# Two heads take turns in the key-value products of a fused attention and MLP kernel, and the second half batch's product moves one step later

## The chip, the cores and the metric

The kernel runs on one core of a Trainium2 chip. The metric is the device time of one execution in microseconds, taken as the median of several runs; lower is better.

## The reference, cut to what matters

Three stages follow one another: a linear attention (softmax over the features of q, softmax over the sequence of k, no product of q with k), a gated MLP with an RMS norm ahead of it, and a second MLP with a rational activation. Shapes: 4 batches, 8 heads, 576 tokens, head size 64; 2304 tokens of width 512; hidden widths 1536 and 2048; all float32.

```python
q_s = softmax(q, axis=-1)                      # over the 64 features of a head
k_s = softmax(k, axis=2)                       # over the 576 tokens
kv  = np.einsum('bhsd,bhse->bhde', k_s, v)     # 64 x 64 for each head: the products of this change
x   = np.einsum('bhsd,bhde->bhse', q_s, kv)    # 2304 x 512 in the end
xn  = x / rms(x) * rms_g
x   = (silu(xn @ w_gate) * (xn @ w_val)) @ w_out
h   = x @ w_in2
out = (P(h) / Q(h)) @ w_out2                   # P, Q: polynomials in h and |h|
```

## The kernel before, in words

The 2304 tokens are cut into six chunks of 384 (numbers c = 0 to 5). The 576 tokens of a batch are laid over 64 partitions times 9 slices, and two heads share the 128 partitions: head h = 0 has partitions 0 to 63, head h = 1 has partitions 64 to 127. A half batch (j = 0 or 1) is four heads: two groups g of two heads h.

**The product.** `kv_pe` makes the four 64x65 results of a half batch (64 columns of v and a column of ones that gives the sum for the softmax). Each is a sum over the 9 slices c, so a product has 2 x 2 x 9 = 36 matmuls of 64 rows, 64 weight columns and 65 moving columns. Both heads write the same PSUM bank, head 0 its partitions 0 to 63, head 1 its partitions 64 to 127. A float32 matmul leaves two records in the trace, so a product shows as x72. `kv_norm` on the VectorE (DVE) then divides by the sums (`rc` is their reciprocal). There are eight products: `akv0`, `akv1` (batch 0) and `bkv0`, `bkv1` (batch 1) in the opening, and two each named `kv_3` and `kv_4` (batches 2 and 3).

**The opening** (about the first 160 us: chunk 0, the loading and splitting of weights, and the attention of chunk 1) runs in the order of a list of names, `ORDER`; each name issues the instructions of one event. The splitting of a weight block into two parts is the work of the lines L169, L174 and L176 (exponents and low words), L183 (`raw`), L190 (`tmp`), L200, L202 and L208 (`w`). The lines `w2` in the list issue two matmuls on an identity (`warm`).

**Chunks 1 to 5** of the first MLP run 12 steps f each: `u_step` issues `g` (12 matmuls), then the events of position 3f, then `vv` (12 matmuls) and the elementwise `product` (u, and its two parts uh by ScalarE and ul by DVE), the events of position 3f + 1, then `y` of the step before (12 matmuls, `emit_y`), then the events of position 3f + 2. While chunk c is worked on, `schedule(c + 1)` puts the attention of the next chunk into these positions; the tuple behind `enumerate` has for each half batch the positions of its maximum, turn, subtraction, exponential and product. Chunk 3 needs batch 2 and chunk 4 needs batch 3, so chunks 2 and 3 have two products each; the other chunks have none there. At position 3 of the tuple, 10, come the exponentials of k and q; at 13 and 15 DVE makes the sums of q (`sumq`) and the normalised q (`qn`); from 18 on q is turned on TensorE (`xq`, which reads `qn`), and from 20 on multiplied with kv (`xx`; the first two use the first half batch's kv, the last two, at 24 and 26, the second's).

All v tiles of the half batches 1 to 3 share one buffer: `load_v(b, 1)` is issued when the first half batch's product has read it. The pool `pw` has four PSUM banks, which g, vv, the products, xq and xx take in turn. Weights for the second MLP are also split in these steps (`stage`, lines L169, L230, L183, L190, L241 and L242).

**After chunk 5** comes the second MLP (`h` and `o` matmuls, 96 steps), bound to TensorE.

Of the kernel before, what the change touches and what calls it, by code (L numbers as in the profile page):

```python
# [47 lines left out]
def kernel(  # L48
# [17 lines left out]
    B, H, S, D = q.shape  # L66
# [5 lines left out]
    SC = S // D  # L72
# [222 lines left out]
    def new_batches(c):  # L295
        return [b for b, off, s, n in runs(c) if s == 0]
# [15 lines left out]
    def load_v(b, j, t=None):  # L312
        t = vt0 if t is None else t
        for g in range(2):
            nc.sync.dma_start(out=t[:, g, :, 0:D], in_=half(v, b, j)[:, g])
        vtl[b, j] = t
# [61 lines left out]
    def kv_pe(b, j, kp):  # L378
        kt, vt = ktl.pop((b, j)), vtl.pop((b, j))
        for g in range(2):  # L380
            for h in range(2):
                r = slice(h * D, (h + 1) * D)
                for c in range(SC):
                    nc.tensor.matmul(
                        kp[r, g * VW:(g + 1) * VW], lhsT=kt[r, g, c], rhs=vt[r, g, c],
                        start=(c == 0), stop=(c == SC - 1),
                    )
# [20 lines left out]
    def q_max(c):  # L408
        mq = at.tile([P, H, TT, 1], F32, tag="mq", name=f"mq_{c}")
        nc.vector.tensor_reduce(out=mq, in_=st["q", c], axis=AX.X, op=ALU.max)  # L410
        st["mq", c] = mq
# [4 lines left out]
    def q_sub(c, eng, i=0, n=1):  # L416
        qt = half_q(st["q", c], i, n)
        eng.tensor_tensor(
            out=qt, in0=qt, in1=half_q(st["mq", c], i, n).to_broadcast(list(qt.shape)), op=ALU.subtract
        )  # L420

    def q_exp(c):
        nc.scalar.activation(st["q", c], st["q", c], AF.Exp)

    def q_sum(c):
        sq = at.tile([P, H, TT, 1], F32, tag="sumq", name=f"sumq_{c}")
        nc.vector.tensor_reduce(out=sq, in_=st["q", c], axis=AX.X, op=ALU.add)
        nc.vector.tensor_scalar_add(sq, sq, 1e-9)
        nc.vector.reciprocal(sq, sq)
        st["sumq", c] = sq  # L430

    def q_norm(c, eng, i=0, n=1):
        if ("qn", c) not in st:
            st["qn", c] = big_tile(F32, xtag[c][0], f"qn_{c}").rearrange(
                "p (t h d) -> p t h d", t=TT, h=H
            )
        qt = half_q(st["q", c], i, n)
        eng.tensor_tensor(
            out=half_q(st["qn", c].rearrange("p t h d -> p h t d"), i, n), in0=qt,
            in1=half_q(st["sumq", c], i, n).to_broadcast(list(qt.shape)), op=ALU.mult,  # L440
        )
# [88 lines left out]
    def rms_wide_pe(c, rp):  # L530
        nc.tensor.matmul(rp[:, :T], lhsT=ones, rhs=st["acc", c], start=True, stop=True)

    def rms_wide(c, rp):
        nv, r, t = (at.tile([P, T], F32, tag=tag, name=f"{tag}w_{c}") for tag in ("sq", "acc", "qT"))
        nc.vector.tensor_scalar(
            out=nv, in0=rp[:, :T], scalar1=-0.5 / DM, scalar2=-0.5e-6, op0=ALU.mult, op1=ALU.add
        )
        nc.vector.tensor_scalar(out=r, in0=nv, scalar1=-2.0, scalar2=None, op0=ALU.mult)
        nc.vector.tensor_scalar(
            out=r.bitcast(I32), in0=r.bitcast(I32), scalar1=-0.5, scalar2=1597463007.0,  # L540
            op0=ALU.mult, op1=ALU.add,
        )
        for _ in range(3):
            nc.vector.tensor_tensor(out=t, in0=r, in1=r, op=ALU.mult)
            nc.vector.tensor_tensor(out=t, in0=t, in1=nv, op=ALU.mult)
            nc.vector.scalar_tensor_tensor(
                out=r, in0=t, scalar=1.5, in1=r, op0=ALU.add, op1=ALU.mult
            )
        st["rms", c] = r
# [26 lines left out]
    def x_norm(c, rp, eng=nc.vector):  # L576
        x_scale(c, 0, rp)
        for p in range(1, KD):
            x_scale(c, p, rp)
            x_rest(c, p - 1, eng)  # L580
        x_rest(c, KD - 1, eng)

    def with_bank(evs, name):

        t = ps(name)
        for pe, _ in evs:
            pe(t)
        for _, rest in evs:
            rest(t)

    def k_events(b, j):
        e = {}
        e["max"] = lambda: k_max(b, j)
        e["turn"] = (lambda t: k_turn_pe(b, j, t), lambda t: k_turn(b, j, t))
        e["sub"] = (lambda t: k_sub_pe(b, j, t), lambda t: k_sub(b, j, t))
        e["exp"] = lambda: k_exp(b, j)
        e["kv"] = (lambda t: kv_pe(b, j, t), lambda t: kv_norm(b, j, t))
        return e

    def x_events(c, p, qT=None):  # L600
        return (
            (lambda t: q_turn_pe(c, p, t), lambda t: q_turn(c, p, t, qT)),
            (lambda t: x_pe(c, p, t), lambda t: x_out(c, p, t)),
        )

    def schedule(c):

        at_pos = [[] for _ in range(NPOS)]

        def put(i, fn):  # L610
            at_pos[i].append(fn)

        def bank(i, ev, name):
            put(i, lambda: with_bank([ev], f"{name}_{c}"))

        eng = nc.gpsimd if c < 2 else nc.vector
        for b in new_batches(c):
            for j, at_ in enumerate(((0, 4, 7, 10, 14), (2, 5, 9, 10, 17))):
                e = k_events(b, j)
                put(at_[0], e["max"])  # L620
                bank(at_[1], e["turn"], f"kt{j}")
                bank(at_[2], e["sub"], f"ks{j}")
                put(at_[3], e["exp"])
                bank(at_[4], e["kv"], f"kv{j}")
                if j == 0:
                    put(at_[4], lambda b=b: load_v(b, 1))
        put(3, lambda: q_max(c))
        put(5, lambda: q_sub(c, eng))
        put(10, lambda: q_exp(c))
        put(13, lambda: q_sum(c))  # L630
        put(15, lambda: q_norm(c, eng))
        turns = []
        for p, (i, n) in enumerate(((18, 20), (20, 22), (22, 24), (24, 26))):
            turn, xev = x_events(c, p)
            bank(n, xev, f"xx{p}")
            turns.append((i, turn, f"xq{p}"))
        for i, turn, name in turns:
            bank(i, turn, name)
        bank(28, (lambda t: rms_wide_pe(c, t), lambda t: rms_wide(c, t)), "rp")
        put(31, lambda: x_norm(c, st["rms", c]))  # L640
        return at_pos
# [181 lines left out]
    with tc.manual_schedule():  # L823
# [73 lines left out]
        for c, pre in enumerate("ab"):  # L897
            for j in range(2):
                put(f"{pre}km{j}", k_max, c, j)
                bank(f"{pre}kt{j}", lambda t, c=c, j=j: k_turn_pe(c, j, t))  # L900
                reader(f"{pre}kx{j}", f"{pre}kt{j}", lambda t, c=c, j=j: k_turn(c, j, t))
                bank(f"{pre}ks{j}", lambda t, c=c, j=j: k_sub_pe(c, j, t))
                reader(f"{pre}kd{j}", f"{pre}ks{j}", lambda t, c=c, j=j: k_sub(c, j, t))
                put(f"{pre}ke{j}", k_exp, c, j)
                put(f"{pre}kz{j}", kv_zero, c, j)
                bank(f"{pre}kv{j}", lambda t, c=c, j=j: kv_pe(c, j, t))
                reader(f"{pre}kn{j}", f"{pre}kv{j}", lambda t, c=c, j=j: kv_norm(c, j, t))
            put(f"{pre}lq", load_q, c)
            put(f"{pre}qm", q_max, c)
            put(f"{pre}qe", q_exp, c)  # L910
            put(f"{pre}qs", q_sum, c)
            for i in range(2):
                for key, fn in (("qd", q_sub), ("qn", q_norm)):
                    name = f"{pre}{key}{i}"
                    put(name, fn, c, engine(name, nc.gpsimd, nc.vector), i, 2)
            for p in range(NP):
                bank(f"{pre}xq{p}", lambda t, c=c, p=p: q_turn_pe(c, p, t))
                bank(f"{pre}xx{p}", lambda t, c=c, p=p: x_pe(c, p, t))
# [145 lines left out]
        for s in range(2, len(steps) + 3):  # L1064
            if s < len(steps):
                c, f = steps[s]
# [44 lines left out]
```

## Time and profile before

| what | value |
|---|---|
| median of 3 runs | 998.48 us (998.29 to 1000.58) |
| profiled execution: its own time | 999.16 us |
| profiled execution: span from first to last instruction | 997.4 us |
| TensorE (PE) busy | 955.3 us, 96% |
| DVE busy | 683.4 us, 69% |
| ScalarE (ACT) busy | 579.5 us, 58% |
| mean granted TensorE clock | 0.985 |

PE is the matmul stream and PEld its weight loads, which lie under it. A share over the whole span hides that the stages differ: the chain of work that ended last goes through DVE in the opening and through PE from about 160 us on.

### The profile page before, as it was taken

How to read it: one execution, taken by the hardware profiler on the slowest of the kernel's cores; microseconds unless marked ns; L12 is line 12 of the kernel's file. 1: busy time of each engine (PE TensorE's matmuls, PEld its weight loads, DVE VectorE, ACT ScalarE, POOL GpSimd, SP SyncE). 2: the span in 40 equal slices, each digit the busy share in tenths (PEclk: the TensorE clock that was granted, in tenths of full speed). 3: DMA queues.
4: the chain of work that ended last, by engine and by line, in shares of the span. 5: the costliest groups of instructions: out<-in, count | busy, mean ns of one | idle time of the engine just before them, and what ended most of it. 6: DMA issues, size and time to landing. Idle time of an engine off the chain costs nothing.

```text
span 997.4 us, 14266 instructions
## 1 busy us (share of the span) xinstructions
PE 955.3 (96%) x5408; PEld 896.3 (90%) x5408; DVE 683.4 (69%) x1160; ACT 579.5 (58%) x1069; POOL 230.8 (23%) x208
## 2 busy tenths in 40 slices
PE   8787879999999999999999999999999999999998
PEld 7676769999989999999999998999999999999997
DVE  5799997577655765666650028877777777777776
ACT  2556554553354235435531238888888788878876
POOL 2475545000000000000001212423323324234222
PEclk9999889999998999999999999999999999999999
DMA  8996001455553645443438731010010010100000
GB/s 209 352 314 221 1 1 53 138 169 179 166 151 104 181 161 147 152 155 127 169 136 307 254 128 64 1 64 1 1 64 1 1 64 1 64 1 1 33 1 32
DMA packets 69588, 108.92 MB, mean 109 GB/s; under 512 B 22672, under 2 KB 49296, under 8 KB 69520
## 3 DMA queue, kind: packets, MB, share of 16 engines
q1 hardware_dynamic: 69520, 108.02, 33.7%
q8 instruction: 42, 0.69, 0.3%
q14 instruction: 26, 0.21, 0.1%
HBM read 79.70 MB, written 28.31 MB: 108 GB/s over the span
## 4 chain that ended last, share of the span: by engine, by line
PE 84%; DVE 12%; issue 2%; DMA 2%; ACT 0%; DVEq 0%
PE h L650 7%; PE o L803 7%; PE h L648 7%; PE o L802 7%; PE h L649 7%; PE o L801 7%; PE g L648 4%; PE g L649 4%; PE g L650 4%; PE vv L648 4%; PE vv L649 4%; PE vv L650 4%; PE y L649 4%; PE y L650 4%; PE y L648 4%; DVE raw L183 3%
## 5 line engine op out<-in xcount | busy, mean ns | idle before, releaser
L789 POOL TENSOR_TENSOR gl<-t,gh 128x384 fp32r<-128x384 f32 x94 | 104.5, 1112 | 253.3 <-ACT gh L787 223.0
L650 PE MATMUL h<-y,wf 128*128 128x384 f32 x384 | 129.5, 337 | 0.0
L648 PE MATMUL h<-y,wf 128*128 128x384 f32 x384 | 129.3, 337 | 0.0
L649 PE MATMUL h<-y,wf 128*128 128x384 f32 x384 | 128.9, 336 | 0.0
L762 DVE SCALAR_TENSOR_TENSOR A<-S,absb,A 128x384 f32<-128x384 f32 x96 | 61.6, 641 | 92.9 <-ACT A L752 92.9
L686 ACT ACTIVATE uh<-u 128x384 fp32r<-128x384 f32 x72 | 37.8, 524 | 133.4 <-DVE u L695 114.3
L803 PE MATMUL o<-wf,gl 128*128 128x512 f32 x288 | 114.1, 396 | 0.0
L802 PE MATMUL o<-wf,gh 128*128 128x512 f32 x288 | 113.7, 395 | 0.0
L801 PE MATMUL o<-wf,gh 128*128 128x512 f32 x288 | 112.0, 389 | 0.0
L648 PE MATMUL y<-uh,w 128*128 128x384 f32 x288 | 98.7, 343 | 2.7 <-ACT uh L686 2.7
L649 PE MATMUL y<-ul,w 128*128 128x384 f32 x288 | 96.7, 336 | 3.9 <-DVE ul L691 3.3
L691 POOL TENSOR_TENSOR ul<-u,uh 128x384 fp32r<-128x384 f32 x18 | 19.2, 1065 | 338.8 <-ACT uh L686 338.7
L650 PE MATMUL y<-uh,w 128*128 128x384 f32 x288 | 96.3, 335 | 0.0
L648 PE MATMUL g<-x,w 128*128 128x384 f32 x248 | 87.8, 354 | 3.4 <-DVE w L200 3.1
L650 PE MATMUL g<-x,w 128*128 128x384 f32 x248 | 85.9, 347 | 3.1 <-POOL w L208 3.1
L695 DVE TENSOR_TENSOR u<-u,vv 128x384 f32<-128x384 f32 x60 | 33.0, 551 | 79.4 <-PE vv L650 79.3
L649 PE MATMUL g<-x,w 128*128 128x384 f32 x248 | 85.5, 345 | 0.9 <-DVE x L962 0.9
L702 ACT ACTIVATE u<-g 128x384 f32<-128x384 f32 x60 | 29.3, 488 | 92.1 <-PE g L650 92.0
L183 DVE TENSOR_SCALAR raw<-raw 128x512 uint16<-128x512 uint16 x68 | 60.2, 913 | 24.2 <-ACT raw L230 23.5
L648 PEld LDWEIGHTS h<-y,wf 128*128 128x128 f32 x384 | 72.2, 188 | 4.1
L649 PEld LDWEIGHTS h<-y,wf 128*128 128x128 f32 x384 | 72.1, 188 | 4.0
L648 PE MATMUL vv<-x,w 128*128 128x384 f32 x208 | 70.7, 340 | 1.7 <-DVE u L695 1.7
(205 smaller groups left out, 2430.3 us busy)
## 6 DMA issues: line engine op xcount, KB each, us to landing
wf<-sd SPq DMA_DIRECT2D x48, 512.0 KB, 4.5
sd<-ws SPq DMA_DIRECT2D x32, 512.0 KB, 3.0
raw<-in_moe_w_out_dram SPq DMA_DIRECT2D x28, 512.0 KB, 5.3
raw<-in_moe_w_in_dram SPq DMA_DIRECT2D x16, 512.0 KB, 4.6
raw<-in_moe_w_gate_dram SPq DMA_DIRECT2D x12, 512.0 KB, 9.4
raw<-in_moe_w_val_dram SPq DMA_DIRECT2D x12, 512.0 KB, 10.5
k<-in_k_dram SPq DMA_DIRECT2D x8, 576.0 KB, 6.5
v<-in_v_dram SPq DMA_DIRECT2D x16, 288.0 KB, 6.9
```

The lines of the kernel that those rows point to most:

```text
L183: nc.vector.tensor_scalar(out=h[:, :, 1], in0=h[:, :, 3], scalar1=0x8000, scalar2=None, op0=ALU.bitwise_and)
L648: nc.tensor.matmul(o, lhsT=lh, rhs=rh, start=start, stop=False)
L649: nc.tensor.matmul(o, lhsT=lh, rhs=rl, start=False, stop=False)
L650: nc.tensor.matmul(o, lhsT=ll, rhs=rh, start=False, stop=stop)
L686: nc.scalar.activation(uh, u, AF.Copy)
L695: nc.vector.tensor_tensor(out=u, in0=u, in1=vv[:, :T], op=ALU.mult)
L702: nc.scalar.activation(u, g[:, :T], AF.Silu)
L762: nc.vector.scalar_tensor_tensor(out=out, in0=in0, scalar=scalar, in1=in1, op0=op0, op1=op1)
L789: eng.tensor_tensor(out=r["gl"], in0=r["t"], in1=r["gh"], op=ALU.subtract)
L801: nc.tensor.matmul(o, lhsT=r["gh"][:, ts], rhs=w[:, 0], start=first, stop=False)
L802: nc.tensor.matmul(o, lhsT=r["gh"][:, ts], rhs=w[:, 1], start=False, stop=False)
L803: nc.tensor.matmul(o, lhsT=r["gl"][:, ts], rhs=w[:, 0], start=False, stop=last)
```

## The change

In `kv_pe` the loop over the slices goes outside the loop over the two heads: before, the 9 slices of head 0 come first and then the 9 of head 1; now the heads take turns after each slice. In `schedule` the product of the second half batch goes from position 17 (the end of step 5) to position 20 (the end of step 6).

```diff
     def kv_pe(b, j, kp):
         kt, vt = ktl.pop((b, j)), vtl.pop((b, j))
         for g in range(2):
-            for h in range(2):
-                r = slice(h * D, (h + 1) * D)
-                for c in range(SC):
+
+            for c in range(SC):
+                for h in range(2):
+                    r = slice(h * D, (h + 1) * D)
                     nc.tensor.matmul(
                         kp[r, g * VW:(g + 1) * VW], lhsT=kt[r, g, c], rhs=vt[r, g, c],
                         start=(c == 0), stop=(c == SC - 1),
...
-            for j, at_ in enumerate(((0, 4, 7, 10, 14), (2, 5, 9, 10, 17))):
+            for j, at_ in enumerate(((0, 4, 7, 10, 14), (2, 5, 9, 10, 20))):
```

The order of the 36 matmuls inside a product doesn't show in the rows below, since all have one line and one pair of tiles. The other edit does. On PE, in chunk 2 around steps 5 to 7, there stood before (the last matmul of y for step 4, the product of the second half batch, the first of g for step 6, then the first turn of q, the first of vv for step 6; then the last of y for step 5, the first product with q, the second turn of q, and g of step 7):

```order
L650 MATMUL y_3_2339<-uh_4_2519,w_819 128x384
L384 MATMUL kv_3_2648<-v_86,k_1_2232 64x65 x36
L648 MATMUL g_6_2695<-x_2_2152,w_862 128x384
...
L446 MATMUL xq_3_2710<-ident,qn_2607 128x128 x3
L648 MATMUL vv_6_2721<-x_2_2152,w_885 128x384
...
L650 MATMUL y_3_2339<-uh_5_2628,w_897 128x384
L465 MATMUL xx_3_2755<-qT_0_2714,kv_0_2580 128x384
L446 MATMUL xq_3_2761<-ident,qn_2607 128x128 x3
L648 MATMUL g_7_2770<-x_2_2152,w_922 128x384
```

The same stretch of PE at its end now (lines are one higher in the changed file):

```order
L651 MATMUL y_3_2339<-uh_5_2628,w_897 128x384
L385 MATMUL kv_3_2711<-v_86,k_1_2232 64x65 x36
L466 MATMUL xx_3_2755<-qT_0_2670,kv_0_2580 128x384
L447 MATMUL xq_3_2761<-ident,qn_2607 128x128 x3
L649 MATMUL g_7_2770<-x_2_2152,w_922 128x384
```

The product moved past g, the first xq, vv and y of step 6, and now stands directly ahead of the first xx.

On DVE in the same place (qn, then the split of a weight block, u and ul of step 5, the norm of the second product in three rows, and the split, u and ul of step 6) there stood before:

```order
L438 TENSOR_TENSOR qn_2607<-q_2228,sumq_2523 128x8x3x64
L242 TENSOR_TENSOR ws_2609<-tmp_2590,ws_2609 128x512
L695 TENSOR_TENSOR u_5_2605<-u_5_2605,vv_5_2614 128x384
L691 TENSOR_TENSOR ul_5_2630<-u_5_2605,uh_5_2628 128x384
L400 TENSOR_SCALAR rc_1_2687<-kv_3_2648 128x2
L401 RECIPROCAL rc_1_2687<-rc_1_2687 128x2
L404 TENSOR_TENSOR kv_1_2685<-kv_3_2648,rc_1_2687 64x2x64 x2
L183 TENSOR_SCALAR raw_2529<-raw_2529 128x512
```

and now:

```order
L439 TENSOR_TENSOR qn_2607<-q_2228,sumq_2523 128x8x3x64
L242 TENSOR_TENSOR ws_2609<-tmp_2590,ws_2609 128x512
L696 TENSOR_TENSOR u_5_2605<-u_5_2605,vv_5_2614 128x384
L692 TENSOR_TENSOR ul_5_2630<-u_5_2605,uh_5_2628 128x384
L183 TENSOR_SCALAR raw_2529<-raw_2529 128x512
...
L692 TENSOR_TENSOR ul_6_2693<-u_6_2664,uh_6_2691 128x384
L401 TENSOR_SCALAR rc_1_2750<-kv_3_2711 128x2
L402 RECIPROCAL rc_1_2750<-rc_1_2750 128x2
L405 TENSOR_TENSOR kv_1_2748<-kv_3_2711,rc_1_2750 64x2x64 x2
```

The norm moved behind ul of step 6; qn, u and ul of step 5 keep their order. Chunk 3 changes in the same way. ScalarE and the DMA queue of SyncE keep their order.

## Rows read from the trace of the kernel before

**Rows 1.** The page's fourth part: the chain that ended last, by engine.

```profile
PE 84%; DVE 12%; issue 2%; DMA 2%; ACT 0%; DVEq 0%
```

**Rows 2.** The chain from 10 to 36 us: start, duration, what.

```profile
15.03 6.88 PE akv L384 x72
...
23.05 6.88 PE akv L384 x72
```

**Rows 3.** Timeline of DVE, 4 to 40 us; in brackets idle before, and releaser.

```profile
29.97 0.16 DVE L400 TENSOR_SCALAR rc<-akv 128x2 f32<-128x2 f32 x1 [5.47 <-PE akv L384]
```

**Rows 4.** Waits of DVE, 28 to 165 us: total, times, longest.

```profile
DVE rc L400 <- PE akv L384: 5.5, 1, 5.5
...
DVE rc L400 <- PE bkv L384: 0.2, 1, 0.2
```

**Rows 5.** Timeline of the DMA queue of SyncE, 0 to 40 us.

```profile
21.99 0.37 SPq L306 DMA_DIRECT2D k<-in_k_dram  x1
```

**Rows 6.** DMA issues from 22.3 to 22.6 us; last: us to landing.

```profile
raw<-in_moe_w_val_dram SPq DMA_DIRECT2D x1, 512.0 KB, 5.0
```

**Rows 7.** Timeline of ACT: the first use of the block of rows 6.

```profile
38.66 1.29 ACT L169 ACTIVATE raw<-raw 128x512 f32<-128x512 f32 x2
```

**Rows 8.** View of tile kv: count, ns minimum/median/maximum, first and last start.

```profile
L384 PE MATMUL kv<-v,k x288: 216/218/367, 280.9 to 392.8; 64*64 64x65 f32 x144
```

**Rows 9.** Timeline of PE in three short windows inside products (start, length, records).

```profile
280.86 0.33 PE L384 MATMUL kv<-v,k 64*64 64x65 f32 x2
...
281.02 0.69 PE L384 MATMUL kv<-v,k 64*64 64x65 f32 x9
...
281.49 0.68 PE L384 MATMUL kv<-v,k 64*64 64x65 f32 x12
```

**Rows 10.** Timeline of PE in chunk 2: both products, and g of step 7.

```profile
280.86 3.88 PE L384 MATMUL kv<-v,k 64*64 64x65 f32 x72
...
293.11 5.96 PE L384 MATMUL kv<-v,k 64*64 64x65 f32 x72 [1.93 <-DMA v<-in_v_dram]
...
309.10 0.42 PE L648 MATMUL g<-x,w 128*128 128x384 f32 x1
```

**Rows 11.** The same places in chunk 3, first records only.

```profile
377.30 0.39 PE L384 MATMUL kv<-v,k 64*64 64x65 f32 x3
...
389.14 0.35 PE L384 MATMUL kv<-v,k 64*64 64x65 f32 x3 [1.51 <-DMA v<-in_v_dram]
...
400.53 0.42 PE L648 MATMUL g<-x,w 128*128 128x384 f32 x1
```

**Rows 12.** Chunk 4, without products: g of step 5, first xq, g of step 7.

```profile
466.30 0.33 PE L648 MATMUL g<-x,w 128*128 128x384 f32 x1
...
474.62 0.27 PE L446 MATMUL xq<-ident,qn 128*128 128x128 f32 x1
...
480.01 0.42 PE L648 MATMUL g<-x,w 128*128 128x384 f32 x1
```

**Rows 13.** Busy time by stretch: length, PE, PEld, DVE, ACT, POOL, granted clock, DMA.

```profile
48.51:51.92 3.41, 3.41 (x12) 3.07 (x10) 3.27 (x5) 1.25 (x3) 2.37 (x2) 0.50 1.08 367
...
294.27:304.50 10.23, 10.23 (x73) 10.01 (x69) 3.63 (x9) 2.57 (x6) 0.00 (x0) 0.50 0.28 105
...
387.30:391.00 3.70, 2.19 (x39) 1.90 (x40) 3.63 (x5) 0.63 (x1) 0.00 (x0) 1.00 0.71 114
```

**Rows 14.** Timeline of DVE: the normalised q in chunks 2 and 3.

```profile
292.09 1.75 DVE L438 TENSOR_TENSOR qn<-q,sumq 128x1536 f32<-128x1536 f32 x1
...
388.54 1.75 DVE L438 TENSOR_TENSOR qn<-q,sumq 128x1536 f32<-128x1536 f32 x1
```

**Rows 15.** Waits of DVE, 282 to 297 us.

```profile
DVE raw L183 <- ACT raw L230: 5.5, 1, 5.5
```

**Rows 16.** Timeline of PE: the gap ahead of the first stretch of rows 13.

```profile
47.52 0.59 PE L552 MATMUL arb<-acc,ones 128*128 128x384 f32 x1 [2.78 <-DVE acc L522]
```

## The prediction

> **What bounds the kernel now.** I read the chain of waits first. Over the span it is 84% PE and 12% DVE [rows 1], but it is not one chain of one kind: up to about 160 us it runs through DVE, later through PE alone. So a product is worth something different in each stage, and I looked at the eight products one by one.
>
> In the opening, the two products of batch 0 are themselves the chain: 6.88 us each, with two short warm-up matmuls between [rows 2]. DVE stands still until the second one ends [rows 3], and that is its last long wait: in the list of its waits from 28 to 165 us this one has 5.5 us, and the second product of batch 1 has 0.2 [rows 4]. From 30 us on DVE is simply full of work. What lets it begin earlier moves the whole opening, unless something else then comes late. The first candidate is the DMA. The queue of SyncE stands until the first product has read its k tile, and then issues at 21.99 us [rows 5]. The weight block issued right after it takes 5.0 us to land [rows 6], so it is there at about 27.4 us, and its first use is at 38.66 us [rows 7]: 11 us to spare. The queue's own restart also moves forward with the first product.
>
> In chunks 2 and 3 PE is the bound, and the places to look at are the two second products. Each waits for its v tile, 1.93 us in chunk 2 and 1.51 us in chunk 3 [rows 10, 11]. In chunk 2 the wait is followed by 10.23 us in which the granted clock is 0.50, that is 1.2 instead of 2.4 GHz, with PE busy all the time [rows 13]. That stretch costs about 5.1 us and is why the second product takes 5.96 us and not 3.88. After the wait in chunk 3 the clock stays full [rows 13].
>
> **What the turns change.** A product leaves 72 records of 0.22 us each that overlap [rows 8]. In the middle of a head's 18 records, 9 records take 0.69 us, so they start (0.69 - 0.22) / 8 = 0.059 us apart; in an equally short window at the change from head 0 to head 1 there are 12 [rows 9]. Three more have found room: at the change the last records of one head run beside the first of the other. There are three such changes, hence 9 hidden records, and (72 - 9) x 0.059 + 0.22 = 3.9 us is just the length of 3.88 us [rows 10]. So the heads' records run side by side wherever neighbours belong to different heads, each head at its own spacing of 0.059. Taking turns makes that true everywhere: 36 spacings instead of 63, 27 x 0.059 = 1.6 us less, minus one spacing at the start, 1.53 us. A product then takes about 2.35 us; its tail lies under the next matmuls, so I count a slot of 2.3. In the opening all lasts 6.88 / 3.88 = 1.8 times as long [rows 2, 10], so there the gain is 2.8 us.
>
> A rule speaks against this. The Trainium skill, TensorEngine Tiling, section "Gotcha 1: PSUM Pressure", says that different row tiles cannot access the same PSUM bank simultaneously, and the two heads do share a bank here. By that rule there would be no overlap and the time would be that of the rival "turns without overlap" below. The 12 records against 9 [rows 9] are two row tiles in one bank and speak against it; they lie in different partitions of the bank, which the section does not discuss.
>
> **The sum, part by part.**
>
> Opening: both products of batch 0 are on the chain, 2 x 2.8 = 5.6 us. The second one's data are early, since the chain reaches it through the first one and the warm-up alone [rows 2]. Behind it DVE takes up all 5.6 us. Of batch 1, DVE does not wait for the first product, and of the second only DVE's 0.2 us counts [rows 4]. Sum 5.8 us.
>
> Chunk 2, from the start of the first product (280.86) to g of step 7 (309.10) [rows 10]. Without products this stretch is known from chunk 4: 474.62 - 466.30 = 8.32 us from g of step 5 to the first xq, and 480.01 - 474.62 = 5.39 us from there to g of step 7 [rows 12]. Now: first product 2.3, then 8.32, so PE reaches the first xq at 291.5. Here a new wait appears. xq needs qn, which DVE finishes at 292.09 + 1.75 = 293.84 [rows 14], and PE does not set that time: DVE waits 5.5 us for ScalarE's exponentials and weight words ahead of it, and not for PE [rows 15]. Before, the second product and its wait lay over it. So PE stands 2.3 us, and in-order behind xq stand vv and y of step 6 and the product. From 293.9 on: 5.39 + 2.3, and g of step 7 starts at 301.6 instead of 309.10. That is 7.5 us less: two shorter products, the 1.93 us and the slow stretch gone, less the 2.3 us.
>
> The moved product waits for nothing of its own: its v was there at 293.11 [rows 10], and it now comes after 298. Its norm on DVE moved behind u and ul of step 6, which gain by it; its reader is xx at position 24, more than a step later. Banks: vv of step 7 now takes the product's, an xx, an xq and a g after it; if the norm is later than that, PE waits for the rest.
>
> Chunk 3: 377.30 + 2.3 + 8.32 = 387.9, qn is there at 388.54 + 1.75 = 390.29 [rows 11, 14], a wait of 2.4 us; then 390.35 + 5.39 + 2.3 = 398.0 against 400.53: 2.5 us less.
>
> Sum: 5.8 + 7.5 + 2.5 = 15.8 us. Everything behind is PE work without a further wait, so it carries to the end.
>
> Clock: two new waits of 2.3 and 2.4 us lie between those of the trace that left the clock alone (1.51 [rows 11, 13]) and one that a slow stretch followed (2.78 us, then 3.41 us at 0.50 [rows 13, 16]). A slow stretch of 3.41 us in dense matmuls costs 1.7 us. I take one of the two: 15.8 - 1.7 = 14.1 us. The bounds are none (15.8) and two (12.4).
>
> The profiled execution has 999.16 us, so 985.1; the median of the runs is 0.7 us lower, so **984.4 us**.
>
> **The rivals.**
>
> *Part of the gain.* The first two records of a product take 0.33 us [rows 9], so they are 0.11 apart, 0.05 more than the rest: TensorE pays on coming to a new tile. If each turn of two records pays this although the heads overlap, a head's 18 turns cost 0.9 us: the gain shrinks to 0.65 us, and in the opening to about 1.2. Opening 2.4 + 0.2; the first products' shares go into the xq waits, which end at the same time, so chunks 2 and 3 lose 0.9 each: 6.6 and 1.6. Together 10.8, less 1.7 for the clock: 989.4. For it: the 0.33. Against it: the 12 records, where the second head had just begun.
>
> *Turns without overlap.* All 72 records in a row: 72 x 0.059 + 0.22 = 4.5 us, 0.6 more than now, in the opening 1.0 more. Opening 2.0 worse; chunk 2: slot 4.4, xq at 293.6, hardly a wait, g at 293.9 + 5.39 + 4.4 = 303.7, gain 5.4; chunk 3: 400.1, gain 0.4. Together 3.8: 994.7. Against it: rows 9.
>
> *Slower.* No overlap, and each of the 36 turns a product pays the 0.05 as well: 4.5 + 36 x 0.05 = 6.3 us, in the opening 11.3. Opening 2 x 4.4 = 8.8 worse, and the second product of batch 1 another 2.2; chunk 2: 280.86 + 6.2 + 8.32 + 5.39 + 6.2 = 307.0, gain 2.1; chunk 3: 403.4, 2.9 worse. Sum 11.8 worse: 1010. It decides from a product of about 5.0 us at full clock on, where the opening's loss (2 x 2.0 us, and 0.9 for batch 1) eats the 4.7 us that chunk 2 then still gains.
>
> *Opening hidden.* The 5.6 us are lost to something that now comes late in the opening: 990. Against it: rows 4 and 7.
>
> *Faster clock.* Two heads at once make TensorE busier in the opening; if it goes at full speed from the second product on, that product saves another 1.8 us and the turns of q over 1 us: 981.5. Nothing in the trace shows it.
>
> **How the numbers follow.** My forecast (full overlap, none to two slow stretches: 982.7 to 986.1) has 0.66; part of the gain 0.12; opening hidden 0.06; faster clock 0.06; turns without overlap 0.06; slower 0.04. The range of 980.5 to 990.5 takes in all but the last two. A measurement here can tell about 0.3%, 3 us, from no change: 995.5 is the border. Faster has 0.66 + 0.12 + 0.06 + 0.06 and half of "without overlap" (994.7 is just under the border), 0.92 after rounding down; the same 0.04; slower 0.04.
>
> **What would show it.** Right: every product near 2.35 us at full clock and near 4 us in the opening; rc of the second product at about 24.4 us; no wait of a product for v; a wait of PE for qn of 2 to 2.5 us ahead of xq in chunks 2 and 3; PE's stretches from the first product to g of step 7 of about 20.7 us in both. Wrong: products of 3 us or more; DVE waits between 25 and 135 us that are not there now; slow stretches of 10 us behind the new waits, as one of the old waits had, at 3.4 us more each.

## The result, and the profile after

The changed kernel takes 980.9 us (median of 4 runs, 980.03 to 983.68) against 998.38 us (4 runs, 997.35 to 1000.58): a ratio of 0.9827, with a 95% interval of 0.9801 to 0.9852. That is 17.5 us less; 14.1 were forecast. The profiled execution has 980.75 us and a span of 979.0 us, so 18.4 us less than the span before (997.4) have to be found.

The chain that ended last, by engine (the page's fourth part), is much the same mix as in [rows 1], but for a new 3% through the DMA queue of SyncE (SPq):

```profile
PE 81%; DVE 11%; SPq 3%; DMA 2%; issue 2%; ACT 1%; DVEq 0%
```

These 3% lie in the opening, from 18.8 to 48.0 us. With the transfer of a weight block behind them, to 56.2 us, the chain there is followed back through the loading of weights and no longer through DVE. A second profiled execution of the same kernel (experiment 6) has such a transfer in its chain too, from 67.0 to 77.3 us; the kernel before has none in its opening. The lists of waits name no engine that waits for a weight block between 15 and 165 us. So the weights seem to arrive about as late as they are needed now; whether they would hold up a still shorter opening is not shown.

**The opening.** The timeline of PE from 12 to 30 us shows the two products of batch 0 and what stands between and behind them, to be read against [rows 2]:

```profile
14.77 3.72 PE L385 MATMUL akv<-v,k 64*64 64x65 f32 x72
18.42 0.71 PE L839 MATMUL warm<-ident 128*128 128x128 f32 x4
19.06 2.32 PE L385 MATMUL akv<-v,k 64*64 64x65 f32 x72
21.31 1.68 PE L447 MATMUL axq<-ident,qn 128*128 128x128 f32 x12
```

The first product is 3.2 us shorter, the second 4.6, and they are not equally long. The busy time by stretch (length, PE, PEld, DVE, ACT, POOL, granted clock, DMA share, GB/s) says why:

```profile
14.80:17.86 3.06, 3.06 (x58) 3.06 (x58) 2.72 (x4) 2.83 (x5) 0.12 (x1) 0.50 1.10 324
17.86:21.20 3.34, 3.34 (x96) 3.15 (x94) 2.47 (x5) 0.95 (x2) 3.04 (x3) 1.00 0.51 111
```

The granted clock goes from 1.2 to 2.4 GHz at 17.86 us, within the first product. Before, both products lay at 1.2 GHz. That is read from their length: the view by stretch prints 1.00 for them, but the trace of the kernel before has no clock record ahead of a rise at 34.86 us (so its mean of 0.985 is too high), and 6.95 us by the timeline is the length that experiment 2 has at a recorded 0.50. On DVE (timeline, 0 to 40 us) the norm of the second product no longer waits:

```profile
18.54 0.16 DVE L401 TENSOR_SCALAR rc<-akv 128x2 f32<-128x2 f32 x1 [0.95 <-PE akv L385]
...
19.64 1.85 DVE L183 TENSOR_SCALAR raw<-raw 128x512 uint16<-128x512 uint16 x1
...
22.25 0.16 DVE L401 TENSOR_SCALAR rc<-akv 128x2 f32<-128x2 f32 x1
```

It stands at 22.25 us instead of 29.97 [rows 3], with no idle time in brackets: the product had ended at 19.06 + 2.32 = 21.38, and DVE was busy with a weight block. The waits of DVE up to 165 us, summed, are in the kernel before and in this one:

```profile
DVE rc L400 <- PE akv L384: 9.6, 2, 5.5
```

```profile
DVE rc L401 <- PE akv L385: 1.0, 1, 1.0
```

So 8.6 us of waiting are gone. About 1.1 of them went into the 1.85 us of `raw` at 19.64 (the next such operation, at 23.34 us, took 0.76 us).

**Chunk 2.** The timeline of PE, in pieces: first product, first turn of q behind its new wait, the moved product, g of step 7; the counterparts are [rows 10].

```profile
271.79 2.32 PE L385 MATMUL kv<-v,k 64*64 64x65 f32 x72
...
284.95 0.52 PE L447 MATMUL xq<-ident,qn 128*128 128x128 f32 x3 [2.13 <-DVE qn L439]
...
289.59 2.32 PE L385 MATMUL kv<-v,k 64*64 64x65 f32 x72
...
292.83 0.42 PE L649 MATMUL g<-x,w 128*128 128x384 f32 x1
```

Both products take 2.32 us. The wait for v is gone, and PE now waits 2.13 us for the normalised q. From the first product to g of step 7 it is 292.83 - 271.79 = 21.04 us; it was 28.24. How the records lie side by side shows in the middle of the first product, in a window of 0.35 us like the two of [rows 9] that had 9 and 12 records:

```profile
272.02 0.75 PE L385 MATMUL kv<-v,k 64*64 64x65 f32 x20
```

There are 20 now. By the order of the code half of them belong to each head, and ten records in 0.75 us start (0.75 - 0.22) / 9 = 0.059 us apart: the old spacing, in both heads at once. Behind the wait for qn the clock stayed full (busy time by stretch):

```profile
284.90:292.90 8.00, 7.95 (x105) 7.34 (x105) 5.35 (x12) 4.67 (x9) 0.00 (x0) 1.00 0.60 199
```

**Chunk 3** is a copy: first product at 361.06, g of step 7 at 382.10, again 21.04 us against 23.23 [rows 11].

```profile
361.06 0.33 PE L385 MATMUL kv<-v,k 64*64 64x65 f32 x4
...
382.10 0.42 PE L649 MATMUL g<-x,w 128*128 128x384 f32 x1
```

The new wait, summed over both chunks, in the list of PE's waits:

```profile
PE xq L447 <- DVE qn L439: 4.3, 2, 2.1
```

The differences: chunk 2 gives 28.24 - 21.04 = 7.2 us, chunk 3 gives 2.2 us. The first product of chunk 2 starts 280.86 - 271.79 = 9.1 us earlier, which is all that the opening gave. 9.1 + 7.2 + 2.2 = 18.5, the span's 18.4 but for rounding. About 5.1 of the 7.2 us are the long slow stretch of [rows 13], which other executions of the kernel before may not have (see the last section).

### The profile page after: what moved, and what is told of

Its sections match the earlier page's. It is cut to its first block, busy times and chain, and to the rows that moved or that the text cites. A ratio compares the mean times of both kernels' runs of the same rounds, so it can differ in the third digit from the quotient of the medians.

```text
span 979.0 us, 14267 instructions
## 1 busy us (share of the span) xinstructions
PE 929.8 (95%) x5408; PEld 871.1 (89%) x5408; DVE 683.6 (70%) x1160; ACT 579.8 (59%) x1069; POOL 231.6 (24%) x208
## 4 chain that ended last, share of the span: by engine, by line
PE 81%; DVE 11%; SPq 3%; DMA 2%; issue 2%; ACT 1%; DVEq 0%
PE h L651 7%; PE h L649 7%; PE o L804 7%; PE o L803 7%; PE h L650 7%; PE o L802 7%; PE vv L649 4%; PE vv L650 4%; PE vv L651 4%; PE y L651 4%; PE y L649 4%; PE y L650 4%; PE g L649 4%; PE g L651 4%; PE g L650 4%; DVE raw L183 3%
## 5 line engine op out<-in xcount | busy, mean ns | idle before, releaser
L649 PE MATMUL g<-x,w 128*128 128x384 f32 x248 | 86.6, 349 | 3.1 <-DVE w L200 3.1
L651 PE MATMUL g<-x,w 128*128 128x384 f32 x248 | 84.8, 342 | 3.4 <-POOL w L208 3.4
L650 PE MATMUL g<-x,w 128*128 128x384 f32 x248 | 84.3, 340 | 0.0
L183 DVE TENSOR_SCALAR raw<-raw 128x512 uint16<-128x512 uint16 x68 | 63.5, 962 | 25.1 <-ACT raw L230 24.6
```

Source lines behind the costliest of these rows:

```text
L183: nc.vector.tensor_scalar(out=h[:, :, 1], in0=h[:, :, 3], scalar1=0x8000, scalar2=None, op0=ALU.bitwise_and)
L649: nc.tensor.matmul(o, lhsT=lh, rhs=rh, start=start, stop=False)
L650: nc.tensor.matmul(o, lhsT=lh, rhs=rl, start=False, stop=False)
L651: nc.tensor.matmul(o, lhsT=ll, rhs=rh, start=False, stop=stop)
```

## The experiments

The theory was that both edits pay and do so apart: the turns by running the heads side by side, and in the opening by bringing up the clock as well; the move by trading the wait for v for a shorter wait for qn. The rivals were that only one of the edits matters, that the early clock has another cause, and that the clock's behaviour behind a wait depends on what follows it.

**1. The turns alone.** The moved product goes back.

```diff
-            for j, at_ in enumerate(((0, 4, 7, 10, 14), (2, 5, 9, 10, 20))):
+            for j, at_ in enumerate(((0, 4, 7, 10, 14), (2, 5, 9, 10, 17))):
```

> The heads take turns, the second half batch's product stays at position 17. Theory A (each edit is worth what its stage's waits say): the opening gains its 9 us as in the changed kernel; in chunks 2 and 3 the first product is 1.5 us shorter, v lands no earlier, so the second product waits about 3.4 and 3.0 us instead of 1.9 and 1.5, a slow stretch of the clock follows at both places (1.7 us or more each), and the time is 984 to 988 us. Theory B (the move is worth nothing, one wait took another's place): 980.9 us within 1.5, and no slow stretch.

Measured: 985.49 us (984.13 to 986.17), ratio 0.9875 (0.9846 to 0.9904). The list of PE's waits between 150 and 450 us has the wait for v back, and longer than before (1.93 and 1.51 us), since PE reaches the product sooner while the DMA brings v at its own time:

```profile
PE kv L385 <- DMA v<-in_v_dram: 6.4, 2, 3.2
```

At the end of each of the two waits the granted clock is 0.50 for one stretch of 3.41 us:

```profile
284.22:287.63 3.41, 3.09 (x57) 3.12 (x59) 2.79 (x4) 1.18 (x4) 0.00 (x0) 0.50 0.29 103
376.38:379.79 3.41, 3.41 (x70) 3.41 (x68) 2.33 (x4) 1.57 (x3) 0.00 (x0) 0.50 0.44 155
```

The turns alone are worth about 13 us, most of it in the opening. In chunk 2 they save 4.9 us (23.39 us from the first product to g of step 7, against 28.24), mainly because the slow stretch is 3.41 and not 10.23 us long; in chunk 3 they save nothing (23.57 us against 23.23).

**2. The move alone.** The loops of before, the product at position 20.

```diff
-            for c in range(SC):
-                for h in range(2):
+            for h in range(2):
...
+                for c in range(SC):
```

> The product moves to position 20, the heads stay one after the other. Theory A: the opening is as before (the second product of batch 0 is normalised at about 30 us); in chunk 2 the v wait and the slow stretch of 10 us go, a wait for the normalised q of about 0.9 us comes ahead of the first turn of q in chunks 2 and 3; gain 6.0 + 1.0 us: 991.4 us. Theory B (the gain is all from the turns): 998 us. Theory C (the opening's early full clock was chance of the execution and not the turns): the opening of this run is also several us shorter than before, second norm at 25 us or earlier.

Measured: 992.33 us (991.62 to 993.55), ratio 0.9941 (0.9922 to 0.9961), so some 6 us. The opening is that of before. The timeline of PE has both products at the old length, and the busy time by stretch has the old clock:

```profile
14.86 6.95 PE L384 MATMUL akv<-v,k 64*64 64x65 f32 x72
...
22.89 6.95 PE L384 MATMUL akv<-v,k 64*64 64x65 f32 x72
```

```profile
14.86:34.33 19.47, 19.47 (x165) 18.09 (x165) 9.24 (x19) 6.80 (x12) 4.74 (x4) 0.50 0.82 243
```

PE is busy for the whole of these 19.47 us and stays at 1.2 GHz. In chunks 2 and 3 the wait for qn is shorter than in the full change, since the first product is longer:

```profile
PE xq L446 <- DVE qn L438: 1.5, 2, 0.8
```

No slow stretch follows, and the twelve executions lie close together (991.62 to 993.55 us), where those of the kernel before beside them go from 993.94 to 1004.08. The two edits alone give about 13 and 6 us, together 17.5: nearly a plain sum.

**3. Turns in batch 0 only**, product at position 17, so that only the opening has them.

```diff
-            for c in range(SC):
-                for h in range(2):
+            turns = [(c, h) for c in range(SC) for h in range(2)]
+            if b > 0:
+                turns = [(c, h) for h in range(2) for c in range(SC)]
+            for c, h in turns:
...
-            for j, at_ in enumerate(((0, 4, 7, 10, 14), (2, 5, 9, 10, 20))):
+            for j, at_ in enumerate(((0, 4, 7, 10, 14), (2, 5, 9, 10, 17))):
```

> The heads take turns in the two products of batch 0 only, the product stays at 17. Theory A (the opening's 9.1 us come from these two products alone, 5.6 from their length and the rest from the clock that is full from the second one on): 989.3 us, second norm at about 22 us, chunks 2 and 3 as before with a v wait of 1.9 and 1.5 us. Rival (the clock was chance): gain 5.6 us, 992.8 us, second norm at about 24.4 us. Rival (batch 1's products give part of the opening's gain): 991 us or more with the second norm at 22 us.

Measured: 989.57 us (985.83 to 991.34), ratio 0.9913 (0.9881 to 0.9944). In the profiled execution the first product of chunk 2 starts at 271.1 us, 9.8 us earlier than before, and the span is 987.5 us, 9.9 less: the opening and nothing else. The norm of the second product stands about where the full change has it (timeline of DVE):

```profile
21.87 0.16 DVE L404 TENSOR_SCALAR rc<-akv 128x2 f32<-128x2 f32 x1
```

The long slow stretch of before [rows 13] is still there, but now in chunk 3 and not in chunk 2, behind a wait of 1.63 us; the wait of 1.67 us in chunk 2 had none:

```profile
375.53:385.77 10.24, 10.24 (x77) 10.03 (x76) 4.20 (x10) 2.24 (x5) 0.00 (x0) 0.50 0.29 104
```

**4. The second product of batch 0 without turns**, all else as changed. This separates "the first product's turns bring the clock up" from "each product is fast by its own turns".

```diff
-            for c in range(SC):
-                for h in range(2):
+            turns = [(c, h) for c in range(SC) for h in range(2)]
+            if (b, j) == (0, 1):
+                turns = [(c, h) for h in range(2) for c in range(SC)]
+            for c, h in turns:
```

> The changed kernel, but the second product of batch 0 has the heads one after the other. Theory A (the turns in the first product bring TensorE to its full clock at about 18 us, and it keeps it): the second product takes 3.9 us, its norm is at about 23.9 us against 22.25, and the opening loses 1.6 us of its 9.1: 982.5 us. Rival (the second product itself must be in turns for the full clock): 6.9 us, norm at about 27 us, 985.5 us or more.

Measured: 982.71 us (981.84 to 983.07), ratio 0.9823 (0.9787 to 0.9859). The timeline of PE:

```profile
14.96 3.92 PE L388 MATMUL akv<-v,k 64*64 64x65 f32 x72
...
19.45 3.88 PE L388 MATMUL akv<-v,k 64*64 64x65 f32 x72
```

The second product has the old order and takes exactly the old full-clock length [rows 10]. The clock becomes full at 18.47 us, inside the first product as in the changed kernel. So of the 4.56 us by which the changed kernel shortens this product, 3.0 are the clock (6.88 to 3.88), which comes with the turns of the product ahead of it, and 1.56 are its own turns. The two waits for qn (2.13 us each) are here, and no slow stretch follows either.

**5. Turns of three slices** in place of one: is the depth of the turn important?

```diff
-            for c in range(SC):
-                for h in range(2):
+            for c, h in [(c, h) for s in range(0, SC, 3) for h in range(2) for c in range(s, s + 3)]:
```

> The changed kernel, but a head has three slices (six records) before the other's turn. Theory A (at a change of head the next head's records can start up to three ahead of their place in the order, as the trace of before showed at its three changes): 11 changes in a product hide 33 records, so a product has 39 spacings of 0.058 us, 2.5 us against 2.32 with turns of one slice and 3.88 without; time within 1.5 us of 980.9. Rival (only direct neighbours overlap, and each change pays 0.05 us for coming to a new tile): 72 - 11 spacings plus 0.55 us, 4.1 us a product, 990 us.

Measured: 983.82 us (983.13 to 984.61), ratio 0.9835 (0.9793 to 0.9877). The product costs little more (timeline of PE):

```profile
19.66 2.48 PE L385 MATMUL akv<-v,k 64*64 64x65 f32 x72
```

0.16 us a product is too little for the 2.9 us. What differs besides are two slow stretches of 3.41 us, one behind each wait for qn (2.10 us each), where the profile of the changed kernel had none (busy time by stretch):

```profile
285.03:288.44 3.41, 3.41 (x13) 3.41 (x14) 2.21 (x4) 2.40 (x5) 0.00 (x0) 0.50 0.62 202
377.19:380.60 3.41, 3.41 (x12) 3.41 (x12) 2.00 (x3) 2.61 (x6) 0.00 (x0) 0.50 0.89 308
```

The first product of chunk 2 starts at 271.79 us, as in the changed kernel, and from there to g of step 7 it is 22.76 us in chunk 2 and again in chunk 3, 1.72 more than 21.04. Twice that is the 3.4 us by which the span is longer (982.4 against 979.0). At half clock, 3.41 us of matmuls cost about 1.7 us.

**6. The changed kernel once more**, to see whether that is a matter of the kernel or of the execution.

> The changed kernel once more, beside the two below on one chip. Theory A: 981 us when no slow stretch follows the two waits for qn, 1.7 us more for each that does (up to 984.3); the profile shows which. Rival (the 2.9 us that turns of three cost are not the clock): no slow stretch here and still 983 us or more.

Measured: 981.44 us (980.77 to 982.04), ratio 0.9836 (0.9823 to 0.985). Its profiled execution took 982.04 us, and it has one slow stretch, behind the wait of 2.12 us in chunk 2, and none behind the equal wait in chunk 3:

```profile
286.02:289.43 3.41, 3.41 (x13) 3.41 (x12) 2.01 (x3) 2.60 (x6) 0.00 (x0) 0.50 0.86 298
382.00:390.00 8.00, 8.00 (x64) 7.89 (x60) 5.59 (x12) 3.77 (x8) 0.00 (x0) 1.00 0.59 201
```

The same kernel thus has none or one. From the first product to g of step 7 it is 22.68 us in chunk 2 and 21.07 in chunk 3: the slow stretch costs 1.6 us, and the 22.76 us with turns of three are the clock but for 0.1. That fits the differences of 1 to 2 us between runs, but the runs without a profile don't show their clock in these stretches.

**7. v by GpSimd's queue.** Here the wait for v is to vanish by another way: the product stays at 17, and v of the second half batches is issued by GpSimd's queue, not behind weight blocks on SyncE's.

```diff
-            nc.sync.dma_start(out=t[:, g, :, 0:D], in_=half(v, b, j)[:, g])
+            queue = nc.gpsimd if b > 1 and j == 1 else nc.sync
+            queue.dma_start(out=t[:, g, :, 0:D], in_=half(v, b, j)[:, g])
...
-            for j, at_ in enumerate(((0, 4, 7, 10, 14), (2, 5, 9, 10, 20))):
+            for j, at_ in enumerate(((0, 4, 7, 10, 14), (2, 5, 9, 10, 17))):
```

> The changed kernel with the product back at 17, and the second half batch's v of batches 2 and 3 loaded from the queue of GpSimd, which stands empty there, instead of from SyncE's queue, where it stands behind a store. Theory A: v is there when the product is reached at about 280.5 us; no wait for v, and the product lies over the wait for the normalised q, so that goes too: about 2.5 us less in each of chunks 2 and 3 than the changed kernel, 976 us. Rival 1 (the wait passes on to u's two parts of step 5, which DVE makes right after): 980 us or more, with a wait of y. Rival 2 (the load takes as long from this queue): v wait of over 1 us, 982 us or more.

Measured: 978.96 us (978.36 to 979.44), ratio 0.9811 (0.9779 to 0.9842). No wait for v, none for qn, no slow stretch; first product to g of step 7 is 291.70 - 271.96 = 19.74 us, against 21.04. The 976 us of the theory were not reached. What is left stands in PE's waits, where the changed kernel has 1.7 us in two waits for u, and this one 2.5 in four:

```profile
PE vv L650 <- DVE u L697: 2.5, 4, 0.8
```

Now that v is early, it is the elementwise work that comes a little late: vv waits for u of the step before. A repeat gave the same:

> The version with the product at 17 and v loaded from GpSimd's queue, once more, to be compared with the changed kernel on the same chip. Theory A: no wait over 1 us in chunks 2 and 3, hence no slow stretch; 2.8 us less than a run of the changed kernel without slow stretches, up to 6 us less than one with two: 978 to 979 us. Rival: the first run's 979.0 was the chip's, no difference to the changed kernel.

Measured: 978.98 us (977.96 to 979.45), ratio 0.9811 (0.9798 to 0.9824).

**8. qn on GpSimd.** The wait for qn could be taken away by giving the normalised q of chunks 2 and 3 to the engine that is idle there.

```diff
-        put(15, lambda: q_norm(c, eng))
+        put(15, lambda: q_norm(c, nc.gpsimd if new_batches(c) else eng))
```

> The changed kernel, but in chunks 2 and 3 the normalised q is made by GpSimd, which has nothing to do there, instead of DVE. Theory A (PE's new wait of 2.1 us ahead of the first turn of q is for this one operation and what stands before it on DVE): GpSimd takes about 2.9 us (two halves of 1.47 in the opening), starts about 2.4 us earlier, so qn is there about 1.1 us earlier; the wait is about 1.0 us in both chunks, time 2.2 us less: 978.7 us. Rival (GpSimd and DVE hinder each other, or the operation is slower there as one piece): the wait is as long as now or longer, 981 us or more.

Measured: 984.88 us (983.4 to 985.98), ratio 0.9845 (0.9815 to 0.9874): by the medians 4 us worse than the change. The intervals of the two ratios overlap, so the reading rests on the profile: from the first product to g of step 7 it is 22.36 and 23.58 us in chunks 2 and 3, against 21.04. PE's waits show a shorter wait for qn and a new one for the high part of u:

```profile
PE y L649 <- ACT uh L687: 3.2, 2, 1.7
PE xq L447 <- POOL qn L439: 1.9, 2, 1.0
```

The timelines of POOL and of DVE show where it comes from:

```profile
281.39 2.76 POOL L439 TENSOR_TENSOR qn<-q,sumq 128x1536 f32<-128x1536 f32 x1 [121.37 <-DVE rc L402]
284.09 0.56 POOL L392 MEMSET kv<- 128x256 f32 x2
```

```profile
282.02 3.23 DVE L183 TENSOR_SCALAR raw<-raw 128x512 uint16<-128x512 uint16 x1
...
287.40 0.56 DVE L696 TENSOR_TENSOR u<-u,vv 128x384 f32<-128x384 f32 x1
```

DVE's `raw` took 0.76 us in the changed kernel; beside POOL's qn it takes 3.23 us, ending 1.1 us after qn does (284.15). So u comes at 287.40 and not at 285.44 (0.36 of these 1.96 us are the later start of the chunk). DVE did not gain the 1.75 us that it handed over. The Trainium skill, SBUF — State Buffer, section "Who interferes with whom", says that DVE and GpSimd share a port pair that one of them holds for a whole instruction while the other stands, and counts tensor_scalar in its faster modes among those that take it. The trace agrees in kind: 284.15 plus 0.76 would be 284.9, and `raw` ended at 285.25. One slow stretch of 3.41 us in chunk 3 (at 380.68) is in the 23.58 us too.

**9. Both together** (v by GpSimd's queue with the product at 17, and qn on GpSimd; the two edits above).

> The version with the product at 17 and v loaded from GpSimd's queue, and in addition qn by GpSimd as in the run beside it. Theory A (what is left of that version's waits in chunks 2 and 3 is vv of step 6 waiting for u of step 5 on DVE, which stands behind qn): these two waits of about 0.7 us go, the short wait of y for ul of step 4 stays; 977.6 us, the shortest of all. Rival (the wait goes to qn, since GpSimd takes longer): 979 us or more.

Measured: 982.58 us (981.5 to 983.87), ratio 0.9823 (0.9793 to 0.9852), by the medians 3.6 us worse than v alone, though these two intervals overlap as well. The theory's 977.6 us fell, for the same reason: DVE's `raw` takes 3.14 us beside POOL's qn here, and the late u now holds up vv, for 5.2 us in all against 2.5.

```profile
PE vv L650 <- DVE u L697: 5.2, 4, 1.9
```

**10. The product at 18**, between the two places tried: behind g of step 6 and ahead of the first turn of q. v comes late for it, but PE would wait for qn right behind it anyway.

```diff
-            for j, at_ in enumerate(((0, 4, 7, 10, 14), (2, 5, 9, 10, 20))):
+            for j, at_ in enumerate(((0, 4, 7, 10, 14), (2, 5, 9, 10, 18))):
```

> The changed kernel with the second half batch's product at position 18, ahead of the first turn of q, and v loaded as before. Theory A: PE reaches the product at about 282.6 us, v's first half lands at about 283.9, so a v wait of about 1.3 us takes the place of the qn wait of 2.1, which lies under the product; about 1 us less than the changed kernel in each of chunks 2 and 3: 978.9 us without slow stretches. Rival (DVE's chain of qn, u and its parts sets the end of the step, wherever the product stands): the same as the changed kernel, with waits of y or vv for u.

Measured: 978.51 us (977.48 to 978.9), ratio 0.9806 (0.9792 to 0.9819). This interval lies below that of the changed kernel on the same chip (0.9823 to 0.985); it has the lowest median, with one number changed, and can't be told from the version with v by GpSimd's queue. PE's waits and timeline:

```profile
PE kv L385 <- ACT ws L241: 2.1, 2, 1.1
```

```profile
284.31 2.32 PE L385 MATMUL kv<-v,k 64*64 64x65 f32 x72 [1.09 <-ACT ws L241]
286.56 0.55 PE L447 MATMUL xq<-ident,qn 128*128 128x128 f32 x3
```

The two waits of about 2.1 us have become two of 1.1, and the turn of q finds qn ready because the product lies over the rest. From the first product to g of step 7: 292.01 - 272.16 = 19.85 us and 19.79 us, 1.2 less than changed. The releaser in the brackets is not the real one: the v tiles were issued at 278.22 and such a transfer took 6.0 us (rows of SyncE's queue and of the DMA issues), which gives 284.2, and the product starts at 284.31. The operation in the brackets, ScalarE's ws, also ended at 284.2; but in chunk 3 of the kernel before the same product began at 389.14 [rows 11], ahead of the end of that operation (388.65 + 0.63 = 389.28), so it doesn't wait for it.

```profile
278.22 1.95 SPq L315 DMA_DIRECT2D v<-in_v_dram  x2
```

```profile
v<-in_v_dram SPq DMA_DIRECT2D x2, 288.0 KB, 6.0
```

## Why the prediction was right, and what it mis-sized

| term | forecast, us | profiled execution, us |
|---|---|---|
| opening | 5.8 | 9.1 |
| chunk 2 | 7.5 | 7.2 |
| chunk 3 | 2.5 | 2.2 |
| slow clock behind the new waits | -1.7 | 0 |
| sum | 14.1 | 18.4 |

The mechanisms of the turns and of the move were right; the number was so with luck. The forecast's own theory gave 982.7 to 986.1 us, and 980.9 lies outside of it. It lies inside the whole range by 0.4 us, because that range was drawn wide enough for the rivals. Two terms were off the same way: the opening by 3.3 us, and the slow stretch that was counted and didn't come by 1.7.

**The product.** 2.35 us was forecast for the turned product and 2.32 measured, from the 12 records against 9 of [rows 9]. Turns of three (2.48 us) confirm the reading that neighbours from different heads overlap. The rule of the Trainium skill, TensorEngine Tiling, section "Gotcha 1: PSUM Pressure", which the prediction weighed, is not borne out here, where two row tiles write different partitions of one bank: 72 records in 2.32 us. "Part of the gain", "turns without overlap" and "slower" are out.

**Chunks 2 and 3.** The trade was as described: waits for qn of 2.13 and 2.14 us against 2.3 and 2.4 forecast, no wait for v, stretches of 21.04 us where 20.7 were expected. That PE does not set the time of qn holds too: DVE had it 283.06 + 1.75 - 271.79 = 13.0 us after the start of the first product, as before (293.84 - 280.86). The move alone shows it without the turns, the turns alone show the wait for v that it removes.

**The clock behind the waits.** The forecast took one slow stretch of two, 1.7 us. Of the profiled executions with two such waits (2.10 to 2.14 us) the first had none, the repeat one, the one of experiment 4 none, turns of three two. So "none to two" was the right statement and one a fair middle; that the first profile had none was chance as far as these runs show.

**The opening is the term that was mis-sized**, 5.8 us against 9.1. The prediction scaled the saving by 1.8, as if both products stayed at 1.2 GHz (about 4 us each, rc at 24.4 us), and gave 0.06 to "faster clock". It is that rival that happened, and a little earlier than it said, in the first product: rc stands at 22.25 us. It comes with the turns: beside the kernel before, twelve executions were profiled. In the eleven whose first product takes turns (it starts at 14.7 to 15.0 us) the clock goes to full between 16.4 and 19.1 us. In the one with the old order (experiment 2) it is at 0.50 from 13.85 to 34.33 us, and in the kernel before it rises at 34.86 us, although PE worked without a break there too. The second product without turns (experiment 4) shows that the first one's turns suffice. What it is about the turns that brings up the clock, no run separates. The rival's own sum gave the opening 5.8 + 1.8 + 1 = 8.6 us or a little more, near the 9.1 measured; that its 981.5 us in all came so close to 980.9 is partly chance, since it counted the slow stretch of 1.7 us as well.

**The rest of the opening**, from 7.7 us at rc to 9.1 at the end. At `acc` (L522, L523 after) it is already 46.91 - 38.17 = 8.7 us. Between rc and `acc` lie, among others, nine operations on 3 elements a partition (L516 to L518); the timelines of DVE and POOL have, before,

```profile
42.48 1.21 DVE L516 TENSOR_TENSOR rw<-rw 128x3 f32<-128x3 f32 x1
43.73 0.94 DVE L517 TENSOR_TENSOR rw<-rw 128x3 f32<-128x3 f32 x1
44.71 0.92 DVE L518 SCALAR_TENSOR_TENSOR rw<-rw 128x3 f32<-128x3 f32 x1
45.66 0.16 DVE L516 TENSOR_TENSOR rw<-rw 128x3 f32<-128x3 f32 x1
```

```profile
43.64 1.96 POOL L948 TENSOR_TENSOR xs<-xr 128x384 f32<-128x384 f32 x2
```

and after

```profile
34.80 0.92 DVE L517 TENSOR_TENSOR rw<-rw 128x3 f32<-128x3 f32 x1
35.76 0.93 DVE L518 TENSOR_TENSOR rw<-rw 128x3 f32<-128x3 f32 x1
36.72 0.17 DVE L519 SCALAR_TENSOR_TENSOR rw<-rw 128x3 f32<-128x3 f32 x1
```

```profile
34.70 1.96 POOL L949 TENSOR_TENSOR xs<-xr 128x384 f32<-128x384 f32 x2
```

As long as POOL works (on w and then on xs, to 45.60, and to 36.66) such an operation takes 0.92 us or more, then 0.16. They all read two tensors; the one-tensor operations of the same size ahead of them (TENSOR_SCALAR on rw) took 0.15 to 0.45 us beside POOL's work. POOL was done 8.9 us earlier, DVE came to these operations 7.7 us earlier, so three were long before and two now. That fits in time and amount; no run tested it by taking POOL's work away. The last 0.3 us were not followed.

"Opening hidden" is out: all of it reached the end of the opening.

## What to carry to other kernels

Where small matmuls use different parts of the TensorE array, write them in turns: here it cost nothing, took 40% off the product (3.88 to 2.32 us), and in the opening brought the full clock 17 us earlier. When a wait is removed by moving work, look at which wait ends next, and try the places in between: the product fits best where it lies over the part of one wait that the other leaves (978.5 us), not where its own wait is zero (980.9). An engine that looks idle is not free help: the two-input work given to GpSimd slowed DVE by more than it took from it.

## What the runs showed of the hardware that was not expected

- The granted clock stayed at 0.50 for 19.47 us of unbroken matmuls that began with the heads one after the other; with the heads in turns it went to 1.00 at 1.6 to 4.3 us after the start of the first product, in eleven profiles of eleven.
- Waits of 2.10 to 2.14 us are sometimes followed by 3.41 us at 0.50 and sometimes not, in the same kernel. Behind waits of 1.5 to 1.9 us with an un-turned product after them there was either none or a stretch of 10.2 us; in chunks 2 and 3 no slow stretch behind a turned product or large matmuls was longer than 3.41 us. Why one wait is followed by one and its twin is not, stays open.
- The kernel before shows groups of times: of its 37 executions beside the experiments most took 997 to 1001 us, three 994 and six 1003 to 1004.3. The groups lie about 5 us apart, the cost of one stretch of 10.2 us at half clock. That fits one such stretch in most executions, none in some and two in others; only one execution of this kernel was profiled, so it is not shown.
- A DVE operation of 0.76 us took 3.23 us beside one GpSimd operation of 2.76 us, and operations on 3 elements took 0.92 us in place of 0.16.
